# Taking the tail of a convolution out of a gated two-layer product: convolution steps of block i+2 move into the end of block i's second layer

## The chip, the cores and the metric

The kernel runs on one core of one Trainium2 chip. The metric is the device time in microseconds (us) of the whole program, on that core; the kernel before takes 2269.23 us (median of three runs, 2268.99 to 2269.92). In the profile the engines are called PE (TensorE, the matrix products; PEld is its weight load), DVE (VectorE), ACT (ScalarE), POOL (GpSimd) and SP (SyncE, which here issues transfers).

## The reference

A causal convolution over time with 7 taps, whose weights go through a softmax and are shared by the 24 channels of a head, feeds a two-layer network with a hard-swish gate. Everything is float32.

```python
# x: (8, 4096, 192), weight: (8, 7), w_in: (192, 2048), w_out: (2048, 192)
w = exp(weight - max(weight, axis=-1)); w = w / (sum(w, axis=-1) + 1e-9)
x_pad = concatenate([zeros((8, 6, 192)), x], axis=1)
y[b, s, h, :] = sum_k w[h, k] * x_pad[b, s + k, h, :]
h = y.reshape(32768, 192) @ w_in
g = h * clip(h + 3, 0, 6) / 6
out = g @ w_out
```

## The kernel before

**Tiles and blocks.** The 32768 tokens are worked on in 32 blocks of 1024 (`NB = 32`, block 0 apart from the rest). The 192 channels lie on 64 partitions, three channels to each (`K3`), and the block's two groups of 512 tokens lie on the lower and upper 64 partitions, so that x and y are tiles of 128 x 3 x 512. There is one x tile and one y tile (`bufs=1`); block i+2's x is loaded only when the previous block's convolution has read the tile for the last time.

**Convolution.** `conv_jobs(i)` (line 857) gives seven jobs: job 0 is a multiplication on ACT (line 859), jobs 1 to 6 are one multiply-add each on DVE over 128 x 1536 elements (line 861), all into the one y tile. Job k reads what job k-1 has written. Once all seven are done, `split_high` and `split_rest` cut y into three parts (HIGH, LOW, MIX, lines 873 to 878) and `swap_parts` exchanges the partition halves by transfers. The first layer multiplies parts of y with parts of w_in[...].

**First layer** (`first_layer`, line 498). A block has 16 chunks: n = 0 to 7 in the group OWN, 8 to 15 in OTHER. `begin(n)` takes one of four slots of two PSUM banks, issues 12 matmuls (HIGH and LOW) and has ACT scale the banks (line 521). `end(n)` issues the other six (MIX), then ACT computes the clipped part (line 302), DVE multiplies it with the bank's content (the gate, line 306), and the slot goes back to the list. The order on PE is begin 0, begin 1, end 0, begin 2, end 1, begin 3 and so on. Since there are four slots, `begin(n + 2)` can start only when the gate of chunk n - 2 has been computed. After `end(n)` the jobs of `jobs[n]` are issued; `jobs[-1]` stands between `begin(1)` and `end(0)`, which is ahead of the first gate.

**Beside it.** After chunks 1, 3, 5 and 7 POOL computes sums of the gate's results (`small_sums`, line 573); after chunks 9, 11 and 13 it computes larger ones (line 414).

**Second layer** (`second_layer`, line 584). It multiplies g with w_out by a scheme of seven products in place of eight, at two levels. Its order is written out as four streams with a clock: `put(j, cost, fn)` places matmuls, and `do(t, fn)` places work of other engines at time t of the fourth stream's clock. `events` (line 710) sorts all of it, and the engines get it in that order. [...] `second_layer` returns two jobs, `finish(1)` and `finish(0)` (line 718): an addition and a transpose on DVE each, and the stores. They are called `left`, and run as `jobs[-1]` of the next block's first layer.

**The loop** (lines 901 to 921). During block i's first layer the convolution of block i+1 is carried out: job 0 was issued at t = 60 in block i-1's second layer, and jobs 1 to 6 come after chunks 1, 3, 5, 7, 9 and 11. Block 1 has them after chunks 2, 4, 6, 8, 10 and 12, and job 0 after chunk 1. In the second layer of block i `split_high` (t = 13), `split_rest` (15) and `swap_parts` (18) prepare block i+1, and `begin_conv` (20) loads x of block i+2.

Of the kernel before, what the change touches and what calls it, by code (L numbers as in the profile page):

```python
# [25 lines left out]
def kernel(  # L26
# [50 lines left out]
    def load_x(i, dma=nc.sync):  # L77
        x = xs.tile([P, K3, PAD + N], F32, name="x")
        head, lower, upper = x_source(i)
        if head:  # L80
            nc.vector.memset(x[0:D2, :, 0:PAD], 0.0)
        dma.dma_start(out=x[0:D2, :, head:], in_=lower)
        dma.dma_start(out=x[D2:P, :, :], in_=upper)
        return x
# [655 lines left out]
    with tc.manual_schedule():  # L740
# [82 lines left out]
        n = 3  # L823
# [33 lines left out]
        def conv_jobs(i):  # L857
            x = x_tiles.pop(i)
            jobs = [lambda: nc.scalar.mul(y[:], x[:, :, 0:N], c_sb[:, 0:1])]
            for k in range(1, KC):  # L860
                jobs.append(lambda k=k: nc.vector.scalar_tensor_tensor(  # L861
                    out=y[:], in0=x[:, :, k : k + N], scalar=c_sb[:, k : k + 1], in1=y[:],
                    op0=ALU.mult, op1=ALU.add,
                ))
            return jobs
# [33 lines left out]
        S3 = last.tile([P, NP, N], F32, name="s3")[:]  # L899
        p1 = last.tile([DH, N], F32, name="p1")  # L900
        conv = conv_jobs(2)
        left = []
        for i in range(1, NB):
            jobs = {2 * n + 1: [job] for n, job in enumerate(conv[1:])}
            jobs[-1] = left
            if i == 1:
                jobs = {n + 1: job for n, job in jobs.items() if n > 0}
                jobs[1] = conv[:1]
            first_layer(i, jobs)
            conv = []  # L910

            def begin_conv():
                x_tiles[i + 2] = load_x(i + 2)
                conv.extend(conv_jobs(i + 2))

            between = []
            if i + 1 < NB:
                between = [(13, split_high), (15, split_rest), (18, swap_parts)]
            if i + 2 < NB:
                between += [(20, begin_conv), (60, lambda: conv[0]())]  # L920
            left = second_layer(i, between)


# [31 lines left out]
```

## Time and profile before

| | us | where it is read |
|---|---|---|
| device time | 2269.23 | median of three runs |
| span of the profiled execution | 2266.7 | head of the page |
| PE busy | 2252.5 (99%) | page, part 1 |
| DVE busy | 1909.8 (84%) | page, part 1 |
| ACT busy | 1389.4 (61%) | page, part 1 |
| POOL busy | 914.2 (40%) | page, part 1 |
| one convolution tap on DVE, line 861 | 2.09 mean, 186 of them | page, part 5 |
| one gate on DVE, line 306, 128 x 1024 | 1.21 mean, 496 of them | groups by form |
| first layer of block 15 | 34.13 | windows, 1077.35 to 1111.48 |
| second layer of block 15 | 35.47 | windows, 1111.48 to 1146.95 |
| first layer of block 31 | 32.93 | windows, 2190.78 to 2223.71 |

A row of the timeline gives the start, the duration, the engine, the line, the operation with its tiles and how many like it follow each other, and in brackets the idle time in front of it with the instruction that ended it. The windows view gives, for each stretch, its length and the busy time of PE, PEld, DVE, ACT and POOL with the number of instructions. The chain of waits is followed back from the last instruction and says at each time which engine's work the end depended on. TensorE was granted its full clock (0.999) over the span.

### The profile page before, as it was taken

Reading aid. Unit: us, or ns where it says so; the run is one execution under the profiler, and the core shown is the slowest. Engines: PE = TensorE matmul, PEld = TensorE weight load, DVE = VectorE, ACT = ScalarE, POOL = GpSimd, SP = SyncE. Lnnn points to the kernel's source line nnn. Section 1 sums busy time; section 2 is a strip of 40 time slices with the busy share of each in tenths; the row PEclk is TensorE's granted clock in tenths of the full one; section 3 lists DMA queues with packets and bytes.
Section 4 is the critical chain, followed back from the end, with each engine's and each line's share of the span. In section 5 each row is a group of like instructions: output and inputs, shape, how many; then the busy total and the mean of one; then the engine's idle time right before and its main releaser. Section 6 shows DMA issues by size and latency. Waiting matters only on the chain.

```text
span 2266.7 us, 50172 instructions
## 1 busy us (share of the span) xinstructions
PE 2252.5 (99%) x21432; PEld 1517.4 (67%) x21432; DVE 1909.8 (84%) x1636; ACT 1389.4 (61%) x1676; POOL 914.2 (40%) x689
## 2 busy tenths in 40 slices
PE   9999999999999999999999999999999999999998
PEld 5456676666766667666667666676666676666765
DVE  8798888898888988888988889888898888898876
ACT  7457655566655666555766556665567655576654
POOL 2345532355423555224553235542245532455322
PEclk9999999999999999999999999999999999999999
DMA  6334234442244332344422443324434234442232
GB/s 154 71 79 82 46 62 90 82 82 55 53 87 89 76 75 45 74 90 82 83 48 57 89 85 80 63 51 80 89 78 79 45 67 89 83 83 51 54 75 34
DMA packets 254063, 166.57 MB, mean 73 GB/s; under 512 B 208528, under 2 KB 213648, under 8 KB 253840
## 3 DMA queue, kind: packets, MB, share of 16 engines
q1 hardware_dynamic: 235416, 129.53, 27.9%
q0 software_dynamic: 17184, 33.57, 8.6%
q8 instruction: 168, 2.75, 0.5%
q14 instruction: 55, 0.45, 0.1%
q10 hardware_dynamic: 1240, 0.27, 0.1%
HBM read 31.72 MB, written 25.17 MB: 25 GB/s over the span
## 4 chain that ended last, share of the span: by engine, by line
PE 65%; DVE 22%; ACT 5%; issue 2%; ACTq 0%; DVEq 0%
PE psum L609 48%; PE psum L510 17%; DVE y L861 11%; DVE g L306 11%; ACT g L302 3%; ACT psum L521 2%; DVE y L479 0%; DVE y L877 0%; DVE results L458 0%; DVE g L573 0%; DVE results L464 0%; ACTq L521 0%; ACT results L709 0%; DVE p L458 0%; DVEq L464 0%
## 5 line engine op out<-in xcount | busy, mean ns | idle before, releaser
L609 PE MATMUL psum<-g,w_out 128*32 128x512 f32 (+1 forms) x6696 | 968.3, 553 | 0.0
L573 POOL TENSOR_TENSOR s<-g 128x256 f32<-128x256 f32 x248 | 359.8, 1451 | 1211.5 <-DVE g L306 1202.3
L306 DVE SCALAR_TENSOR_TENSOR g<-g,psum 128x1024 f32<-128x1024 f32 (+1 forms) x528 | 605.9, 1180 | 132.7 <-ACT g L302 132.4
L302 ACT ACTIVATE g<-psum,half 128x1024 f32<-128x1024 f32 (+1 forms) x528 | 565.0, 1088 | 0.9
L521 ACT ACTIVATE psum<-psum 128x1024 f32<-128x1024 f32 x496 | 500.3, 1009 | 103.1 <-PE psum L510 98.1
L510 PE MATMUL psum<-y_other,w_in 64*128 64x512 f32 x4464 | 548.3, 394 | 4.4 <-DVE g L306 0.7
L609 PEld LDWEIGHTS psum<-g,w_out 128*32 128x32 f32 x6696 | 367.8, 110 | 249.0 <-issue 127.2
L510 PE MATMUL psum<-y,w_in 64*128 64x512 f32 x4464 | 522.1, 388 | 0.6 <-ACT psum L521 0.4
L510 PEld LDWEIGHTS psum<-y_other,w_in 64*128 64x128 f32 x4464 | 406.8, 184 | 135.9 <-DVE g L306 50.6
L510 PEld LDWEIGHTS psum<-y,w_in 64*128 64x128 f32 x4464 | 413.5, 184 | 117.2 <-issue 26.0
L609 PE MATMUL psum<-s,w_out 128*32 128x512 f32 (+1 forms) x3224 | 465.3, 576 | 0.0
L861 DVE SCALAR_TENSOR_TENSOR y<-x,c_sb,y 128x1536 f32<-128x1536 f32 x186 | 388.0, 2086 | 0.2
L414 POOL TENSOR_TENSOR s<-g 128x1024 f32<-128x1024 f32 x93 | 289.3, 3111 | 2.9 <-DVE g L306 2.9
L609 PE MATMUL psum<-g,w_s 128*32 128x256 f32 x1240 | 282.8, 379 | 0.2 <-DVE p L458 0.2
L609 PEld LDWEIGHTS psum<-s,w_out 128*32 128x32 f32 x3224 | 151.7, 110 | 82.7 <-issue 50.8
L414 DVE TENSOR_TENSOR s<-g 128x2048 f32<-128x2048 f32 (+1 forms) x93 | 187.0, 2038 | 1.1
L609 PEld LDWEIGHTS psum<-g,w_s 128*32 128x32 f32 x1240 | 136.3, 110 | 69.4 <-DVE p L458 1.1
L609 PE MATMUL psum<-s,w_s 128*32 128x256 f32 x744 | 170.7, 379 | 0.0
L573 DVE TENSOR_TENSOR g<-g 128x1024 f32<-128x1024 f32 x124 | 151.7, 1224 | 5.3
L458 DVE TENSOR_TENSOR results<-results 96x512 f32<-96x512 f32 (+1 forms) x32 | 21.4, 670 | 144.7 <-ACT results L709 144.7
L414 DVE TENSOR_TENSOR g<-g 128x2048 f32<-128x2048 f32 x62 | 139.1, 2284 | 0.0
L606 ACT COPY psum<-psum 32x512 f32<-32x512 f32 x93 | 51.2, 551 | 131.9 <-PE psum L609 131.9
(82 smaller groups left out, 1315.2 us busy)
## 6 DMA issues: line engine op xcount, KB each, us to landing
y_other<-y SPq DMA_DIRECT2D x186, 384.0 KB, 5.1
g<-g POOLq DMA_DIRECT2D x62, 512.0 KB, 5.1
out_dram<-results SPq DMA_DIRECT2D x378, 64.0 KB, 2.0
x<-in_x_dram SPq DMA_DIRECT2D x53, 388.5 KB, 7.7
stage<-in_moe_w_in_dram SPq DMA_DIRECT2D x16, 192.0 KB, 4.5
stage<-in_moe_w_out_dram SPq DMA_DIRECT2D x8, 384.0 KB, 5.2
x<-in_x_dram SPq DMA_DIRECT2D x7, 384.0 KB, 8.3
x<-in_x_dram POOLq DMA_DIRECT2D x2, 388.5 KB, 6.3
```

The source lines that it names most:

```text
L302: nc.scalar.activation(r6, h, ACT.Relu, bias=half[:], scale=1.0 / 6.0)
L306: nc.vector.scalar_tensor_tensor(out=g_, in0=g_, scalar=1.0, in1=h, op0=ALU.min, op1=ALU.mult)
L414: engine.tensor_tensor(out=o[:, r], in0=a[:, r], in1=b[:, r], op=op)
L458: nc.vector.tensor_tensor(out=out, in0=x, in1=y, op=op)
L510: nc.tensor.matmul(out=psum[:, 2 * slots[n] + k], lhsT=r32(w_in_parts[part][r, c, s]), rhs=r32(y_other[0][r, part, s] if group else y_own[ ...
L521: nc.scalar.mul(both(n), both(n), 4097.0)
L573: engine.tensor_tensor(out=o, in0=p, in1=q, op=op)
L606: streams[3].append((t - 0.5, lambda: fn(*args, **kw)))
L609: nc.tensor.matmul(out=out, lhsT=w, rhs=x, start=start, stop=True, tile_position=(0, j * QS), skip_group_check=True,)
L861: jobs.append(lambda k=k: nc.vector.scalar_tensor_tensor(out=y[:], in0=x[:, :, k : k + N], scalar=c_sb[:, k : k + 1], in1=y[:], op0=ALU.mu ...
```

## The change

Jobs 1 and 2 of the convolution move from block i+1's first layer to the end of block i's second layer (t = 72 and 73, behind the additions and transposes at t = 62 and 66). Job 3 goes ahead of the first gate of block i+1, behind `finish(1)` and `finish(0)`. Jobs 4, 5 and 6 stay in the first layer, now after chunks 1, 3 and 5. Block 1 has no second layer in front of it: its job 0 is issued before its first layer begins, and jobs 1, 2 and 3 ahead of its first gate. No instruction is added or removed; the purpose is to put convolution steps where DVE has less to do.

```diff
         conv = conv_jobs(2)
-        left = []
+        conv[0]()
+        left = conv[1:3]
         for i in range(1, NB):
-            jobs = {2 * n + 1: [job] for n, job in enumerate(conv[1:])}
-            jobs[-1] = left
-            if i == 1:
-                jobs = {n + 1: job for n, job in jobs.items() if n > 0}
-                jobs[1] = conv[:1]
+            jobs = {2 * n + 1: [job] for n, job in enumerate(conv[4:])}
+            jobs[-1] = left + conv[3:4]
             first_layer(i, jobs)
             conv = []
...
             if i + 2 < NB:
-                between += [(20, begin_conv), (60, lambda: conv[0]())]
+                between += [(20, begin_conv), (60, lambda: conv[0]()), (72, lambda: conv[1]()), (73, lambda: conv[2]())]
             left = second_layer(i, between)
```

## The prediction

> **What bounds the kernel now.** I read the page's first part and its chain of waits, then the windows of one ordinary block and of the last one, then the timelines of the weight loads, of DVE and of POOL in block 15.
>
> ```profile
> PE 2252.5 (99%) x21432; PEld 1517.4 (67%) x21432; DVE 1909.8 (84%) x1636; ACT 1389.4 (61%) x1676; POOL 914.2 (40%) x689
> ...
> PE 65%; DVE 22%; ACT 5%; issue 2%; ACTq 0%; DVEq 0%
> ```
>
> PE is busy 99% of the span, yet the chain that sets the end lies on DVE for 22%: the "busy" of PE contains stretches in which it is paced by others. Which ones, the windows say (first layer of block 15, first layer of block 31):
>
> ```profile
> 1077.35:1111.48 34.13, 34.02 (x290) 26.45 (x289) 29.71 (x23) 30.95 (x32) 24.96 (x19) 1.00 0.14 23
> ...
> 2190.78:2223.71 32.93, 32.93 (x291) 26.75 (x290) 18.56 (x17) 30.96 (x32) 18.69 (x20) 1.00 0.17 29
> ```
>
> Block 31 has the same matmuls, gates and ACT work, but no convolution to do for a next block. It is 1.20 us shorter, and the chain of waits there is one piece of PE work of 32.92 us. So 32.93 us is the first layer with DVE out of the way, and 1.20 us a block is all that the taps can cost. The second layer is 35.47 us in both kinds of block; in the chain it is PE alone, 35.47 us of 216 pieces in block 15. Nothing is to be gained there. The weight loads of block 15 show where PE stops:
>
> ```profile
> 1093.17 1.22 PEld L510 LDWEIGHTS psum<-y_other,w_in 64*128 64x128 f32 x12 [0.27 <-DVE g L306]
> ...
> 1097.61 3.97 PEld L510 LDWEIGHTS psum<-y_other,w_in 64*128 64x128 f32 x36 [0.49 <-DVE g L306]
> 1102.04 3.99 PEld L510 LDWEIGHTS psum<-y_other,w_in 64*128 64x128 f32 x36 [0.45 <-DVE g L306]
> 1106.47 3.95 PEld L510 LDWEIGHTS psum<-y_other,w_in 64*128 64x128 f32 x36 [0.43 <-DVE g L306]
> ```
>
> Four stops, each released by a gate. Counting 12 matmuls to a begin and 6 to an end, they stand ahead of begin 8, 10, 12 and 14, which need the slots of gates 4, 6, 8 and 10. The stops come 4.43 us apart for 36 matmuls. Unhindered, block 31 does 126 loads in 14.24 us, so 36 in 4.07: each of the last three stops costs about 0.35 us, and the first, where the backlog just begins to show, the rest, 1.20 - 3 x 0.35 = 0.15 us. The DVE timeline explains the backlog, and shows the room outside it:
>
> ```profile
> 1072.69 0.71 DVE L464 STREAM_TRANSPOSE results<-p 96x512 f32<-96x512 f32 x1
> 1078.07 0.69 DVE L458 TENSOR_TENSOR results<-results 96x512 f32<-96x512 f32 x1 [4.67 <-ACT results L709]
> ...
> 1080.11 0.71 DVE L464 STREAM_TRANSPOSE results<-results 96x512 f32<-96x512 f32 x1
> 1082.66 1.22 DVE L306 SCALAR_TENSOR_TENSOR g<-g,psum 128x1024 f32<-128x1024 f32 x1 [1.84 <-ACT g L302]
> 1084.60 1.22 DVE L306 SCALAR_TENSOR_TENSOR g<-g,psum 128x1024 f32<-128x1024 f32 x1 [0.72 <-ACT g L302]
> 1085.74 1.81 DVE L861 SCALAR_TENSOR_TENSOR y<-x,c_sb,y 128x1536 f32<-128x1536 f32 x1
> 1087.47 2.38 DVE L306 SCALAR_TENSOR_TENSOR g<-g,psum 128x1024 f32<-128x1024 f32 x2
> 1089.77 2.21 DVE L861 SCALAR_TENSOR_TENSOR y<-x,c_sb,y 128x1536 f32<-128x1536 f32 x1
> ```
>
> Two gates (2.30 us from start to start) and a tap (2.14) take 4.44 us, against 4.07 us of matmuls for two chunks. DVE falls back by some 0.36 us with every tap after the first, and has used up what the four slots allow when gate 4 is due. Ahead of the gates it is idle for 4.67 us (waiting for ACT's last copy of the second layer) and for 1.84 us (waiting for the first clip).
>
> [...]the first of POOL's sums takes 2.25 us where a tap runs and 0.74 us in block 31, and a tap takes 1.81 us where POOL is still, 2.2 us where it has to wait. [...]lines 877 and 479 take 1.75 us and an unhindered tap 1.81 us, which I use. [...]here 34.02 of 34.13 us are "busy" with 1.2 us of stops in them.
>
> **The change part by part.**
>
> *Jobs 1 and 2 to the tail of the second layer.* They stand behind the transpose that ends at 1073.40 and ahead of the addition at 1078.07. Two taps by 1.81 us with POOL still (its next work is at 1085.90) are 3.6 us in a hole of 4.67: done by about 1077.0. Their inputs are there: ACT's job 0 ends at 1069.09, x was loaded from t = 20 on. Behind them on DVE wait finish(1), finish(0) and the first gate; none is moved. Cost 0. PE needs nothing from DVE in this stretch.
>
> *Job 3 ahead of the first gate.* From 1080.82 to about 1082.6, in the 1.84 us hole; the gate could start at 1082.66. If it slips by some tenths, the 0.72 us ahead of the second gate take it in. Cost 0. Even at the longest tap of the trace (2.38 us) three are 7.14 us against 4.67 + 1.84 + 0.72 = 7.23 us.
>
> *Jobs 4, 5, 6 after chunks 1, 3, 5.* In these places DVE has exactly the work it had: a tap of the same size behind gates 1, 3 and 5, with POOL's sums beside it. So gates 4 and 6 come as late as before, and the stops ahead of begin 8 and begin 10 stay (0.15 + 0.35 = 0.50 us). After that no tap comes: gates 8 and 9 follow at once, DVE needs 2.3 us for what PE does in 4.07, and catches up within one pair. The stops ahead of begin 12 and begin 14 go: 2 x 0.35 = 0.70 us a block. First layer: 34.13 - 0.70 = 33.43 us. ACT isn't in the way: its two instructions a chunk follow each other at 1.94 us where PE has been held up (block 1, 111.43 to 113.37), below the 2.04 us of PE.
>
> *Into the second layer.* POOL's later sums are no longer held by taps, so they come earlier; the last gates keep their place relative to PE's last matmul. Cost 0, gain 0.
>
> *The sum for ordinary blocks.* Blocks 2 to 30 do a convolution: 29 x 0.70 = 20.3 us. Block 31 has none before or after.
>
> *Block 1.* Its first layer takes 35.94 us (99.89 to 135.83), 3.0 over the free one. One reason is ACT's job 0 at 108.02 (1.57 us), which stops PE for 0.85 us at 111.56. Job 0 now falls into ACT's idle 10.27 us before 101.60: x was issued at 90.42 and 91.07 and lands 6.3 us later by the page's row, 97.4. The three taps follow DVE's transpose ending at 100.75. POOL runs eight sums of 0.46 us there, so 5.4 to 6.4 us: gate 0 slips from 105.06 to between 106.2 and 107.1, and its end to some 107.8, where an ordinary block's is about 0.6 us earlier. The delay runs through to begin 10: 33.43 + 0.6 = 34.0 us, 1.9 less than before. The second layer has 36.63 us, 1.16 over the ordinary, because POOL's last sums held DVE's at 139.44 for 3.49 us, and PE waited 1.1 us for the addition behind it; with POOL earlier I expect 1.1 of that back. Block 1: 3.0 us, between 1 and 4.
>
> Together 20.3 + 3.0 = 23.3 us: 2269.23 - 23.3 = 2245.9 us.
>
> **Rivals.**
>
> *All stops go* (chance 0.07). If the remaining three taps fell so that POOL doesn't hold them (1.81 in place of 2.2 us), the backlog at gates 4 and 6 would be some 0.8 us smaller and PE would run as in block 31: 30 x 1.20 + 2 = 38 us, 2231. Against it: POOL's sums have the same places after chunks 1, 3 and 5.
>
> *Only one stop goes* (0.08). If DVE were still late for gate 8, one stop of 0.35 us a block would stay: 29 x 0.35 + 2 = 12 us, 2257. Against it: after the tap of chunk 5 two gates are followed by no tap.
>
> *A new wait, slower* (0.07). If a tap at the tail had to wait (for x, for ACT's job 0, or for a transfer that DVE's queue doesn't show now), everything behind it on DVE, the finishing jobs and all gates, would slip, and PE with the gates. The slack is 7.23 - 5.43 = 1.8 us. A wait of 2.8 us would push every gate by 1.0 us: 0.30 us net a block, 29 x 0.30 - 3 = 6 us slower, 2275. For it: x and y have one buffer each. Against it: x is issued 25 us earlier and takes 8 us.
>
> **How the numbers follow.** The first case has the chance 0.78 and gives 2245.9; with its own uncertainty (block 1 by 1 to 4 us, a stop by 0.30 to 0.40 us) 2242 to 2250. The range reaches towards the rivals on both sides: 2238 to 2256. Faster by over 0.2% (below 2264.7) are the first three cases, 0.93; of the last 0.06 are slower and 0.01 within 0.2%.
>
> **What would show it.** Right: the first layer of ordinary blocks at 33.4 us; weight loads stopped by a gate at two places, 16 and 20 us after the block's start, and at none later; two taps of 1.8 us in the hole of 4.67 us and one in that of 1.84; the first gate at the same distance from the block's start (5.3 us); second layer 35.47 us, and 35.5 us in block 1 too. Wrong: stops ahead of begin 12 or 14; a gap in front of a tap in the tail; a first gate over 0.7 us later; a second layer longer than 35.5 us.

## The result and the profile after

The changed kernel takes 2245.91 us (median of four runs, 2245.67 to 2246.07) against 2269.51 us for the kernel before in the same comparison: a ratio of 0.9896, 95% interval 0.9879 to 0.9913. The forecast was 2245.9 us, range 2238 to 2256.

The page of the changed kernel, part 1 and the chain of waits:

```profile
PE 2233.8 (100%) x21432; PEld 1525.2 (68%) x21432; DVE 1890.1 (84%) x1636; ACT 1388.8 (62%) x1676; POOL 825.0 (37%) x689
...
PE 98%; DVE 1%; ACT 0%; issue 0%; DVEq 0%; ACTq 0%
```

The shares of busy time have moved little, but the chain has: DVE had 22% of it and has 1% now. The windows of block 15 (first and second layer), and the first layer of block 31:

```profile
1065.13:1098.59 33.46, 33.42 (x289) 26.61 (x288) 25.78 (x21) 30.94 (x32) 22.90 (x20) 1.00 0.17 29
1098.59:1134.07 35.48, 35.48 (x387) 21.16 (x386) 32.78 (x27) 12.03 (x21) 2.65 (x2) 1.00 0.57 116
2168.07:2201.02 32.95, 32.95 (x290) 26.76 (x289) 18.55 (x17) 30.95 (x32) 18.70 (x20) 1.00 0.17 29
```

The first layer went from 34.13 to 33.46 us, 0.51 above that of block 31; in the second layer DVE does 2.95 us more (32.78 for 29.83), and its length stays. The weight loads of block 15's first layer have two stops left where there were four:

```profile
1065.13 15.55 PEld L510 LDWEIGHTS psum<-y,w_in 64*128 64x128 f32 x138 [0.84 <-issue]
1080.97 1.23 PEld L510 LDWEIGHTS psum<-y_other,w_in 64*128 64x128 f32 x12 [0.28 <-DVE g L306]
...
1085.39 12.13 PEld L510 LDWEIGHTS psum<-y_other,w_in 64*128 64x128 f32 x108 [0.47 <-DVE g L306]
```

From 1085.39 on 108 loads follow each other without a stop. On DVE the three moved taps lie in the two holes:

```profile
1060.47 0.71 DVE L464 STREAM_TRANSPOSE results<-p 96x512 f32<-96x512 f32 x1
1061.11 3.63 DVE L861 SCALAR_TENSOR_TENSOR y<-x,c_sb,y 128x1536 f32<-128x1536 f32 x2
1065.85 0.69 DVE L458 TENSOR_TENSOR results<-results 96x512 f32<-96x512 f32 x1 [1.11 <-ACT results L709]
...
1068.53 1.77 DVE L861 SCALAR_TENSOR_TENSOR y<-x,c_sb,y 128x1536 f32<-128x1536 f32 x1
1070.45 1.22 DVE L306 SCALAR_TENSOR_TENSOR g<-g,psum 128x1024 f32<-128x1024 f32 x1
1072.40 1.22 DVE L306 SCALAR_TENSOR_TENSOR g<-g,psum 128x1024 f32<-128x1024 f32 x1 [0.72 <-ACT g L302]
```

Two taps take 3.63 us of the 4.67, and 1.11 us of waiting for ACT are left. The third fills the 1.84 us, and the first gate starts 5.32 us after the block's first weight load (1070.45 - 1065.13), where it was 5.31 before.

**Where the time came from.** Blocks 2 to 30 together take 1999.1 us (168.97 to 2168.07) instead of 2018.3 (172.45 to 2190.78): 19.2 us. Block 1 takes 69.12 us (99.85 to 168.97) instead of 72.56 (99.89 to 172.45): 3.44 us. Together that is, within 0.1 us, the 22.6 us between the spans of the two profiled executions (2266.7 and 2244.1). The medians are 23.6 us apart: the profiled execution of the kernel before took 2268.56 us, 0.95 us under the median of 2269.51.

### The profile page after: what moved, and what is told of

Its sections match the earlier page's. It is cut to its first block, busy times and chain, and to the rows that moved or that the text cites. A ratio compares the mean times of both kernels' runs of the same rounds, so it can differ in the third digit from the quotient of the medians.

```text
span 2244.1 us, 50173 instructions
## 1 busy us (share of the span) xinstructions
PE 2233.8 (100%) x21432; PEld 1525.2 (68%) x21432; DVE 1890.1 (84%) x1636; ACT 1388.8 (62%) x1676; POOL 825.0 (37%) x689
## 4 chain that ended last, share of the span: by engine, by line
PE 98%; DVE 1%; ACT 0%; issue 0%; DVEq 0%; ACTq 0%
PE psum L609 49%; PE psum L510 44%; PE psum L296 2%; PE psum L341 2%; DVE g L306 1%; DVE y L861 1%; PE psum L755 0%; PE psum L763 0%; ACT g L302 0%; DVE results L458 0%; ACT psum L521 0%; DVE results L464 0%; ACT results L709 0%; DVE zeros L111 0%; DVEq L464 0%
## 5 line engine op out<-in xcount | busy, mean ns | idle before, releaser
L573 POOL TENSOR_TENSOR s<-g 128x256 f32<-128x256 f32 x248 | 318.8, 1285 | 1213.6 <-DVE g L306 1213.6
L510 PE MATMUL psum<-y_other,w_in 64*128 64x512 f32 x4464 | 530.6, 390 | 1.3
L510 PEld LDWEIGHTS psum<-y_other,w_in 64*128 64x128 f32 x4464 | 411.3, 184 | 110.3 <-DVE g L306 22.1
L861 DVE SCALAR_TENSOR_TENSOR y<-x,c_sb,y 128x1536 f32<-128x1536 f32 x186 | 360.5, 1938 | 1.3
L414 POOL TENSOR_TENSOR s<-g 128x1024 f32<-128x1024 f32 x93 | 224.6, 2415 | 67.2 <-DVE g L306 67.2
L414 DVE TENSOR_TENSOR s<-g 128x2048 f32<-128x2048 f32 (+1 forms) x93 | 179.4, 1957 | 1.1
L458 DVE TENSOR_TENSOR results<-psum,results 32x256 f32<-32x256 f32 (+1 forms) x125 | 68.0, 544 | 48.4 <-issue 47.0
```

The source lines that it names most:

```text
L414: engine.tensor_tensor(out=o[:, r], in0=a[:, r], in1=b[:, r], op=op)
L458: nc.vector.tensor_tensor(out=out, in0=x, in1=y, op=op)
L510: nc.tensor.matmul(out=psum[:, 2 * slots[n] + k], lhsT=r32(w_in_parts[part][r, c, s]), rhs=r32(y_other[0][r, part, s] if group else y_own[ ...
L573: engine.tensor_tensor(out=o, in0=p, in1=q, op=op)
L861: jobs.append(lambda k=k: nc.vector.scalar_tensor_tensor(out=y[:], in0=x[:, :, k : k + N], scalar=c_sb[:, k : k + 1], in1=y[:], op0=ALU.mu ...
```

## The experiments

Each ratio is to the kernel before, run in the same comparison (median 2269.6 to 2269.9 us); the 95% interval follows in brackets. Block 15 or 16 stands for the ordinary blocks.

**How many taps leave the first layer, and which stop goes with them.** The theory: the gain doesn't come by the tap, but by the gate behind it. A tap after chunk 3, 5, 7 or 9 delays gate 4, 6, 8 or 10, for which begin 8, 10, 12 or 14 waits. Two kernels move fewer taps (edits against the changed kernel); block 1 is as in the changed kernel in both.

```diff
# two in the tail, none ahead of the first gate, four inside
-            jobs = {2 * n + 1: [job] for n, job in enumerate(conv[4:])}
-            jobs[-1] = left + conv[3:4]
+            inside = conv[4:] if i == 1 else conv[3:]
+            jobs = {2 * n + 1: [job] for n, job in enumerate(inside)}
+            jobs[-1] = left + (conv[3:4] if i == 1 else [])
```

> In blocks 2 to 30 jobs 1 and 2 are in the tail of the second layer, none ahead of the first gate, and jobs 3, 4, 5, 6 after chunks 1, 3, 5, 7; block 1 as in the changed kernel. Theory (a stop belongs to the gates behind a tap after chunks 3, 5, 7 or 9): a third stop comes back, ahead of begin 12; the first layer of an ordinary block is 33.46 + 0.35 = 33.8 us, the kernel 2245.9 + 29 x 0.35 = 2256 us. Rival (every tap taken out is worth the same, 0.65/3 = 0.22 us a block): 33.68 us and 2252 us.

Measured: 2255.66 us, ratio 0.9937 (0.9922 to 0.9952). The weight loads of its block 16:

```profile
1154.42 1.22 PEld L510 LDWEIGHTS psum<-y_other,w_in 64*128 64x128 f32 x12 [0.28 <-DVE g L306]
...
1158.85 3.95 PEld L510 LDWEIGHTS psum<-y_other,w_in 64*128 64x128 f32 x36 [0.48 <-DVE g L306]
1163.28 8.04 PEld L510 LDWEIGHTS psum<-y_other,w_in 64*128 64x128 f32 x72 [0.48 <-DVE g L306]
```

Three stops, the first layer 33.80 us (1138.59 to 1172.39). The tap ahead of the first gate is worth 2255.66 - 2245.91 = 9.8 us, one stop of 0.34 us in 29 blocks.

```diff
# nothing in the tail, one ahead of the first gate, five inside (blocks 2 to 30)
...
+            else:
+                jobs = {2 * n + 1: [job] for n, job in enumerate(conv[2:])}
+                jobs[-1] = left + conv[1:2]
...
-                between += [(20, begin_conv), (60, lambda: conv[0]()), (72, lambda: conv[1]()), (73, lambda: conv[2]())]
+                between += [(20, begin_conv), (60, lambda: conv[0]())]
```

> In blocks 2 to 30 nothing is in the tail, job 1 is ahead of the first gate and jobs 2 to 6 come after chunks 1, 3, 5, 7, 9; block 1 as in the changed kernel. Theory: the tap after chunk 11 that is saved held no gate that a begin waits for, so all four stops stay, the first layer of an ordinary block is 34.1 us as before, and only block 1 gains: 2269.5 - 3.4 = 2266 us. Rival (every tap taken out is worth 0.22 us a block): 33.9 us and 2260 us.

Measured: 2266.15 us, ratio 0.9984 (0.9977 to 0.9991). Block 16's first layer is 34.15 us (1143.69 to 1177.84), with all four stops (0.28, 0.49, 0.46 and 0.47 us of idle time ahead of weight loads). A tap less in the first layer gained nothing in ordinary blocks: the one after chunk 11 stood ahead of gates that no begin of its block waits for. What is gained against the kernel before is block 1's share (next experiment). The rival, an equal worth for every tap, falls in both runs.

**Block 1 alone.** The kernel before, with block 1's arrangement of the changed one:

```diff
-        left = []
+        conv[0]()
+        left = conv[1:3]
...
-            jobs[-1] = left
             if i == 1:
-                jobs = {n + 1: job for n, job in jobs.items() if n > 0}
-                jobs[1] = conv[:1]
+                jobs = {2 * n + 1: [job] for n, job in enumerate(conv[4:])}
+            jobs[-1] = left + (conv[3:4] if i == 1 else [])
```

> The kernel before with block 1's part of the change alone: its job 0 ahead of its first layer, jobs 1, 2, 3 ahead of its first gate, 4, 5, 6 after chunks 1, 3, 5. Theory: block 1 takes 69.1 us in place of 72.6, everything else stays: 2269.5 - 3.4 = 2266.1 us. Rival (the gain of block 1 comes from the later blocks' places): no change.

Measured: 2266.03 us, ratio 0.9983 (0.9976 to 0.9990). Block 1 takes 69.06 us (33.59 and 35.47), 3.5 less than before.

**How much the holes hold.** Three taps in the tail and two ahead of the first gate, one after chunk 11 (edit against the changed kernel, blocks 2 to 30):

```diff
...
+            else:
+                jobs = {11: conv[6:]}
+                jobs[-1] = left + conv[4:6]
...
-                between += [(20, begin_conv), (60, lambda: conv[0]()), (72, lambda: conv[1]()), (73, lambda: conv[2]())]
+                between += [(20, begin_conv), (60, lambda: conv[0]()), (72, lambda: conv[1]()), (73, lambda: conv[2]()), (74, lambda: conv[3]())]
```

> In blocks 2 to 30 jobs 1, 2, 3 are in the tail of the second layer, jobs 4 and 5 ahead of the first gate, job 6 after chunk 11; block 1 as in the changed kernel. This overfills the idle time. Theory (room of 4.67 + 1.84 + 0.72 = 7.23 us): five taps of 1.75 us are 8.7 us, the first gate comes some 2 us later and ends about 1.2 us after begin 4 needs its slot; one stop of 1.3 us there, none later: first layer 34.2 us, about 2268 us. Rival (DVE makes up for it with no taps behind, since PE has two chunks in hand): first layer 32.95 us, 2231 us.

Measured: 2270.09 us, ratio 1.0001 (0.9992 to 1.0009). DVE and the weight loads around the start of block 15's first layer (1075.41):

```profile
1071.38 5.48 DVE L861 SCALAR_TENSOR_TENSOR y<-x,c_sb,y 128x1536 f32<-128x1536 f32 x3
...
1079.45 3.63 DVE L861 SCALAR_TENSOR_TENSOR y<-x,c_sb,y 128x1536 f32<-128x1536 f32 x2
1082.99 2.35 DVE L306 SCALAR_TENSOR_TENSOR g<-g,psum 128x1024 f32<-128x1024 f32 x2
```

```profile
1084.26 8.04 PEld L510 LDWEIGHTS psum<-y,w_in 64*128 64x128 f32 x72 [1.46 <-DVE g L306]
```

The first gate starts 7.6 us after the block's start instead of 5.3, and PE stops once, ahead of begin 4. The first layer is 34.26 us with no further wait for a gate. A late first gate is what the forecast's rival "a new wait, slower" was about; here it comes from too many taps and not from a tap that waits, and it gives back the whole gain.

**Why a tap takes 2.2 us in the first layer.** The second tap of block 15 in the kernel before (2.21 us from 1089.77) starts inside one of POOL's small sums:

```profile
1089.63 0.74 POOL L573 TENSOR_TENSOR s<-g,s 128x256 f32<-128x256 f32 x1
```

Whether these sums lengthen the taps is asked of the kernel before, with zeros written by POOL in place of its small sums (the sums are left out):

```diff
-            engine.tensor_tensor(out=o, in0=p, in1=q, op=op)
+            if engine is nc.gpsimd:
+                engine.memset(o, 0.0)
+            else:
+                engine.tensor_tensor(out=o, in0=p, in1=q, op=op)
```

> The kernel before, with POOL writing zeros where it computed the small sums of the first layer: the sums are left out, the waits and the places stay, but POOL reads nothing from SBUF there. Theory [...]: taps take 1.81 us in place of 2.2, two gates and a tap take 4.04 us against PE's 4.07, the stops nearly vanish: first layer 33.0 us, 2269.5 - 29 x 1.1 - 1 = 2236 us. Rival (a tap takes 2.2 us for another reason, the PSUM or the weights' reads): taps stay at 2.2 us, 2269 us.

Measured: 2233.71 us, ratio 0.9841 (0.9825 to 0.9857). All six taps stay in the first layer, and nearly all of the loss is gone. DVE, and POOL's zeros (the edit adds three lines above the tap, so that it stands in line 864):

```profile
1069.06 1.81 DVE L864 SCALAR_TENSOR_TENSOR y<-x,c_sb,y 128x1536 f32<-128x1536 f32 x1
1070.79 2.38 DVE L306 SCALAR_TENSOR_TENSOR g<-g,psum 128x1024 f32<-128x1024 f32 x2
1073.08 1.81 DVE L864 SCALAR_TENSOR_TENSOR y<-x,c_sb,y 128x1536 f32<-128x1536 f32 x1
1074.81 2.43 DVE L306 SCALAR_TENSOR_TENSOR g<-g,psum 128x1024 f32<-128x1024 f32 x2
```

```profile
1067.47 4.11 POOL L574 MEMSET s<- 128x256 f32 x16 [38.48 <-DMA out_dram<-results]
```

Every tap of the block is 1.81 us, and two gates with a tap come every 4.02 to 4.08 us, at PE's pace (36 loads in 4.07 us in block 31). The first layer of this block is 32.96 us, an estimate from its gates: the first starts at 1065.97, taken as 5.32 us after the layer's start, and gate 13 at 1093.70, taken as 0.09 us after its end, as in the run with 3, 7, 11 below. In the whole execution the weight loads of line 510 wait for a gate three times, 2.5 us in sum. The expectation was wrong in one thing: zeros don't depend on the gates, so POOL didn't keep its places but wrote all sixteen in 4.11 us. From the second tap on POOL was out of the way, until its larger sums, the first of which began at 1085.48, 0.16 us after a tap. Only the block's first tap ran beside POOL's writes, and it took 1.81 us: these writes did not lengthen it. So the run shows that POOL's sums are what lifts DVE over PE's pace; that it is their reading rests on that one tap of a block, and how one engine holds the other is not shown.

**Where the three taps stand that stay.** The changed kernel leaves 0.5 us a block. All of the following differ from it in one line:

```diff
-            jobs = {2 * n + 1: [job] for n, job in enumerate(conv[4:])}
+            jobs = {n: [job] for n, job in zip((9, 11, 12), conv[4:])}
```

with (7, 9, 11), (5, 8, 11), (5, 8, 12) and (3, 7, 11) in the others.

> The changed kernel with jobs 4, 5, 6 after chunks 9, 11, 12 in place of 1, 3, 5. Theory: only one of these taps stands ahead of a gate that a begin waits for (gate 10, begin 14), and with no backlog yet it stops nothing; the last falls into the idle time of DVE ahead of gate 13. First layer 32.95 us as in block 31, second layer 35.47: 2245.9 - 30 x 0.5 = 2231 us. Rival (three taps in the first layer cost 0.5 us wherever they stand): 2246 us. A second rival: the late taps push DVE's work at the start of the second layer, which gets longer than 35.47 us by up to 1 us: 2231 + 30 = 2261 us.

Measured: 2259.7 us, ratio 0.9955 (0.9940 to 0.9969): slower than the changed kernel, as the second rival said. The first layer is 32.98 us (block 15, 1071.47 to 1104.45 in the chain), as in block 31, but the second has 36.4. DVE, POOL and the weight loads at the seam of block 15's layers:

```profile
1103.04 2.83 DVE L861 SCALAR_TENSOR_TENSOR y<-x,c_sb,y 128x1536 f32<-128x1536 f32 x1
1105.80 3.47 DVE L306 SCALAR_TENSOR_TENSOR g<-g,psum 128x1024 f32<-128x1024 f32 x3
```

```profile
1101.23 3.03 POOL L414 TENSOR_TENSOR s<-g 128x1024 f32<-128x1024 f32 x1
```

```profile
1107.06 0.16 PEld L609 LDWEIGHTS psum<-g,w_out 128*32 128x32 f32 x8 [0.81 <-DVE g L306]
```

The tap after chunk 12 met POOL's sum of the pair before, took 2.83 us, and pushed gates 13 to 15 to 1.4 us after the seam; in the kernel before they came 0.1 us after it. For those gates the weight loads of the second layer stand idle for 0.81 us.

> The changed kernel with jobs 4, 5, 6 after chunks 7, 9, 11. Theory: gate 10 stands behind two taps, as gate 4 does in the kernel before, so that one stop of 0.15 us is left ahead of begin 14; first layer 33.1 us, 2245.9 - 30 x 0.35 = 2235 us. Rival (three taps cost 0.5 us wherever they stand): 2246 us.

Measured: 2233.44 us, ratio 0.9839 (0.9823 to 0.9855), as expected: first layer 33.03 us, second 35.47. The first layer is 0.08 us longer than block 31's, by estimate a stop ahead of begin 14, which waits for gate 10: that gate began at 1086.05, 1.18 us later than it would have without a tap.

> The changed kernel with jobs 4, 5, 6 after chunks 5, 8, 11. Theory (a backlog builds up only when a tap comes for every two gates): three gates and a tap are 3 x 1.15 + 2.2 = 5.65 us on DVE against 6.12 us of matmuls for three chunks, so no backlog and no stop at all in blocks 2 to 30; first layer 32.95 us, second 35.47 us, 2231 us. Rival (what counts is only that the taps come late, behind chunk 6): a stop of 0.13 to 0.35 us ahead of begin 10, 2235 to 2241 us.

Measured: 2238.97 us, ratio 0.9864 (0.9849 to 0.9878). The theory missed: there is a stop, though not where the rival put it. The DVE, POOL and weight-load timelines of block 15:

```profile
1083.17 1.22 DVE L306 SCALAR_TENSOR_TENSOR g<-g,psum 128x1024 f32<-128x1024 f32 x1 [0.82 <-ACT g L302]
1084.31 2.33 DVE L861 SCALAR_TENSOR_TENSOR y<-x,c_sb,y 128x1536 f32<-128x1536 f32 x1
1086.57 2.34 DVE L306 SCALAR_TENSOR_TENSOR g<-g,psum 128x1024 f32<-128x1024 f32 x2
```

```profile
1084.29 0.74 POOL L573 TENSOR_TENSOR s<-g 128x256 f32<-128x256 f32 x1
1084.98 2.27 POOL L573 TENSOR_TENSOR s<-g,s 128x256 f32<-128x256 f32 x1
```

```profile
1087.83 5.99 PEld L510 LDWEIGHTS psum<-y_other,w_in 64*128 64x128 f32 x54 [0.38 <-DVE g L306]
```

No backlog stood before this tap: DVE waited 0.82 us for gate 8. But POOL had begun a sum 0.02 us earlier, so the tap took 2.33 us, and gate 9 began 1.36 us later than it would have without a tap (1083.17 + 2.04 = 1085.21). One held tap alone stops PE, ahead of begin 13, which waits for gate 9, and costs 0.25 us a block (first layer 33.20 us). In the run with 7, 9, 11, gate 8 came 0.83 us late behind a tap of 1.81 us and stopped nothing.

> As with chunks 5, 8, 11, but the last tap after chunk 12. Theory for the longer second layer of the kernel with taps after 9, 11, 12 (the tap after chunk 12 is held by POOL's sum of the pair before, and pushes gates 13 to 15, for which PE waits at the start of the second layer): the second layer is again over 35.47 us, by 0.4 to 0.9 us, about 2245 to 2258 us. Rival (it was the crowding of three taps in the last third): second layer 35.47 us, 2231 us.

Measured: 2251.9 us, ratio 0.9920 (0.9904 to 0.9937): in block 15 the second layer is 35.83 us and the first 33.26. DVE and POOL there:

```profile
1099.47 3.11 DVE L861 SCALAR_TENSOR_TENSOR y<-x,c_sb,y 128x1536 f32<-128x1536 f32 x1
1102.51 3.47 DVE L306 SCALAR_TENSOR_TENSOR g<-g,psum 128x1024 f32<-128x1024 f32 x3
```

```profile
1098.08 2.87 POOL L414 TENSOR_TENSOR s<-g 128x1024 f32<-128x1024 f32 x1
```

So the place after chunk 12 is enough to lengthen the second layer, by 0.36 us. It is not all of the 0.93 us of the kernel with 9, 11, 12: there DVE came to this tap only 1.34 us ahead of the seam (1103.04 against 1104.38), behind the tap after chunk 11, and here 2.19 us ahead of it (1099.47 against 1101.66). So the crowding probably has its share.

> The changed kernel with jobs 4, 5, 6 after chunks 3, 7, 11. Theory formed after the run with 5, 8, 11 (a gate may end 1.3 us later than it does unhindered before PE stops; a tap of 1.81 us behind a gate costs 0.9 us of it, one held by POOL, 2.3 us, all of it; POOL's sums begin after odd chunks, so a tap after an odd chunk goes first if POOL has finished the sums before, which takes it under 8 us): three taps of 1.81 us, no stop, first layer 32.95 us, second 35.47, 2231 us. Rival (a tap after chunk 3 or 7 stops PE whatever POOL does): first layer 33.2 us or more, 2239 us.

Measured: 2230.67 us, ratio 0.9828 (0.9811 to 0.9844), faster than both kernels. DVE and POOL in block 15:

```profile
1069.24 1.22 DVE L306 SCALAR_TENSOR_TENSOR g<-g,psum 128x1024 f32<-128x1024 f32 x1 [0.82 <-ACT g L302]
1070.38 1.81 DVE L861 SCALAR_TENSOR_TENSOR y<-x,c_sb,y 128x1536 f32<-128x1536 f32 x1
1072.11 2.44 DVE L306 SCALAR_TENSOR_TENSOR g<-g,psum 128x1024 f32<-128x1024 f32 x2
```

```profile
1070.55 2.25 POOL L573 TENSOR_TENSOR s<-g 128x256 f32<-128x256 f32 x1 [1.08 <-DVE g L306]
```

and the windows of the block's two layers:

```profile
1057.96:1090.91 32.95, 32.95 (x289) 26.76 (x289) 25.18 (x21) 30.95 (x32) 21.79 (x19) 1.00 0.18 30
1090.91:1126.38 35.47, 35.47 (x386) 21.16 (x385) 33.17 (x27) 12.03 (x21) 3.66 (x2) 1.00 0.57 116
```

Here the tap and POOL's sum are released by the same gate, and the tap starts 0.17 us earlier: it takes 1.81 us and POOL's sum 2.25. The first layer is that of block 31, with three taps in it.

## Why the prediction was right

**The bound on the gain.** Block 31's 32.93 us as the length without hindrance is confirmed by the last run: 32.95 us with taps in every block. So is the 35.47 us of the second layer, in every run whose last tap doesn't stand after chunk 12.

**Tail and first gate at no cost.** As forecast: taps of 1.8 us, the first gate in its place. Three taps (3.63 + 1.77 = 5.40 us) fit into the room of 7.23 us; the five of the kernel with five taps ahead (5.48 + 3.63 = 9.11 us) don't, and stop PE. No run tried four. One argument against the rival "a new wait" was misread: x is not issued 25 us ahead of the tap but some 17 to 18 (its two transfers were issued at 1042.68 and 1044.34, the first tap in the tail began at 1061.11). That is still over twice the 7.7 us that it takes to land, and no tap waited.

**Two stops stay, two go.** Shown stop by stop in the weight loads, and by the kernels with four and five taps inside. Forecast were 0.70 us a block; measured are 34.13 - 33.46 = 0.67 in block 15 and 19.2 / 29 = 0.66 on average, in sum 19.2 us instead of 20.3.

**Block 1.** Forecast 3.0 us, measured 3.44. The first layer gained 2.29 (forecast 1.9), the second 1.15 (1.1). ACT's job 0 ran at 97.57, released by x's landing, as worked out. The three taps took 5.87 us (5.4 to 6.4), and gate 0 began at 106.42 (106.2 to 107.1). What I had not seen is that there the taps held POOL as well: three of its sums of 0.46 us took 1.97, 1.85 and 1.98. Nor did the first layer go as worked out. Its weight loads:

```profile
99.85 7.39 PEld L510 LDWEIGHTS psum<-y,w_in 64*128 64x128 f32 x66 [0.84 <-ACT y L859]
107.68 3.96 PEld L510 LDWEIGHTS psum<-y,w_in 64*128 64x128 f32 x36 [0.44 <-DVE g L306]
111.84 3.96 PEld L510 LDWEIGHTS psum<-y,w_in 64*128 64x128 f32 x36 [0.21 <-DVE g L306]
...
120.27 12.15 PEld L510 LDWEIGHTS psum<-y_other,w_in 64*128 64x128 f32 x108 [0.39 <-DVE g L306]
```

PE stops ahead of begin 4, 6 and 10. The forecast had the delay of the first gates run through to begin 10 on top of the stops ahead of begin 8 and 10; the one ahead of begin 8 isn't there, probably because PE was late already by the first two and the tap after chunk 3 was not held (1.80 us at 112.84, with POOL's first small sum only at 113.07). Two of its readings were wrong as well. An ordinary block's first gate ends 6.53 us after the block's start, so that a gate ending at 107.8 (7.91 us after it) would be 1.4 us late and not 0.6; 0.6 fits the second gate, which came 0.44 us late. And the 0.85 us ahead of 111.56 are idle time of the weight loads; the matmuls waited 0.43 us.

**How near the sum came.** The two misses, 1.1 us too much for the ordinary blocks and 0.4 too little for block 1, partly cancel, and the medians differ by 1.0 us more than the profiled spans. That the median met the forecast to 0.1 us is chance to that extent.

**What the forecast did not know.** Its account of the stops was a backlog, 0.36 us with every tap after the first. That describes the kernel before, but is not the whole rule: a first tap held by POOL (2.33 us, gate 1.36 us late) is enough, while a tap of 1.81 us (gate 0.83 us late) is not. How late a gate may come follows from two runs: with 5, 8, 11, gate 9 came 1.36 us late and PE lost 33.20 - 32.95 = 0.25 us; with 7, 9, 11, gate 10 came 1.18 us late (1086.05 against 1078.75 + 3 x 2.04) and PE lost 33.03 - 32.95 = 0.08. In both, PE lost what went beyond 1.1 us (the expectation for 3, 7, 11 had put this at 1.3). The forecast's rival "all stops go" had the right cause, POOL, and was rightly held improbable, since this change leaves two of the three taps where POOL's earlier sums are still running: they take 2.23 and 2.24 us, the first 1.81.

## What to carry to other kernels

Find out how late a result may come before the critical engine stops, and count the work ahead of each such result, not the work in total: here one tap moved was worth nothing, two 0.33 us a block and three 0.67. A block that lacks the work in question (the last one) gives the most that can be won before anything is tried. Where two engines hold each other, as here (a tap of 2.33 us behind a sum, a sum of 2.25 us behind a tap), place the instruction on which the path depends so that both are released by the same event and the other engine has finished what it had: three taps after chunks 3, 7, 11 cost nothing (32.95 us, as block 31) where the same three after 1, 3, 5 cost 0.5 us (33.46 us).

## What the runs showed of the hardware

**Which of the two is held.** Here it is the one that starts later, down to small differences: the tap that starts 0.17 us ahead of POOL's sum takes 1.81 us and the sum 2.25 (with 3, 7, 11); the one that starts 0.02 us behind it takes 2.33 us and the sum 0.74 (with 5, 8, 11). The tap beside POOL's zeros took 1.81 us.

**How long a held tap takes.** I had not expected how exactly it follows from what POOL has left. After chunk 8 POOL's sum had 0.72 us to go when the tap began (1084.29 + 0.74 - 1084.31), and the tap took 0.52 us more than 1.81; with 9, 11, 12, after chunk 12, it was 1.22 us to go (1101.23 + 3.03 - 1103.04) and 1.02 us more, and with 5, 8, 12 it was 1.48 us to go (1098.08 + 2.87 - 1099.47) and 1.30 us more. A held tap of the kernel before agrees: that at 1089.77 found 0.60 us left (1089.63 + 0.74 - 1089.77) and took 0.40 us more. Each of these four taps lost what POOL's instruction had left, less some 0.2 us; what the 0.2 us are is not shown.

**The order on DVE.** The gates that come late stand behind a late tap in the order of issue. DVE kept that order in block 15 of the changed kernel: the third tap's input y was ready at 1064.74 (1061.11 + 3.63), but DVE was idle for 1.11 us until the addition issued ahead of it could start at 1065.85, and took the tap at 1068.53.
